# k of units 4 to 11 loaded in natural order and transposed by the DMA crossbar from SBUF to SBUF; the first unit's casts on VectorE; a new order by swaps

## The chip, the core and the metric

The kernel runs on one core of a Trainium2 chip. The metric is the device time of one execution in microseconds (us), as the median of several runs. Engines are named as in the profile: PE is TensorE's matmuls (PEld its weight loads), DVE is VectorE, ACT is ScalarE, POOL is GpSimd, and SP (SyncE) issues nearly all DMAs.

## The reference

Sliding-window attention with four sink positions, followed by a channel mix. The batch is 4, with 8 heads, 768 positions and a head size of 64; the mix works on 512 channels with 1024 hidden ones.

```python
scores = scale * np.matmul(q, k.transpose(0, 1, 3, 2))
keep = is_sink | in_window            # 4 sinks, window of 128
a = softmax(np.where(keep, scores, -1e9))
x = np.matmul(a, v)                   # heads side by side: [B, S, 512]
xk = mu_k * x + (1 - mu_k) * x_prev   # x_prev: one position earlier
xr = mu_r * x + (1 - mu_r) * x_prev
out = sigmoid(xr @ w_r) * (np.maximum(xk @ w_k, 0) ** 2 @ w_v)
```

## The kernel before

The work is cut into 12 units of 256 positions: unit u is batch u // 3, third T = u % 3. All matmuls are in bf16.

`load` brings k, q and v of a unit into SBUF in float32. k and q come as one DMA of 512 KB, with two neighbouring positions (j = 0, 1) side by side on a partition; unit 0's come as two DMAs of 256 KB. v comes as two DMAs of 256 KB in natural order, 128 positions on the 128 partitions.

`prepare` works on halves of four heads. k is cast to bf16 on ACT (`kb`), q on DVE (`qb`), by the table `CAST`. PE then makes four transposes of 128 x 128 into a PSUM bank (line 519), and ACT copies them from there into `kt` or `qt`, putting the positions back in order (line 527). v is cast on POOL (on DVE in unit 0) into `vb`. For the first unit of a batch, POOL copies the sink keys out of `kt`, and PE and DVE prepare the sink values.

`attend` makes two pairs of scores per unit (line 602), ACT takes the exponential (`e`, line 622), DVE applies the mask (line 636), PE multiplies by the values (lines 647 and 659), and DVE divides into `x`. A pair of scores reads the half of `kt` and `qt` with its heads, and that of the unit before. `mix` transposes x on PE (line 698), ACT copies it out (`xt`, line 704), and DVE makes `xk` and `xr`. `ffn` has, per unit, eight groups of key matmuls (line 740), ACT's relu (`rl`, line 749), the square on DVE (`kk`), two gates (line 763) with ACT's tanh (`th`), four groups of products (line 778), DVE's last step (`ob`, line 787) and two stores (line 794).

Each operation is recorded in a `Plan` with an engine, a planner's cost, what it reads and writes, and the buffers it takes and holds. The table `ORDER` lists, for each engine, the numbers of its operations in the order in which they are issued; numbers count the operations as they are recorded. `schedule` walks through those lists, hands out the buffers (three tiles of `kt`, two of `kb`, three of `ks`, four banks), and puts dummy matmuls (fills, line 798) into PE's queue up to a planned time of 45 us where it plans a gap. Every engine works through its list in order, so an instruction that waits holds up all behind it. SP's list holds the loads and the stores.

Of the kernel before, what the change touches and what calls it, by code (L numbers as in the profile page):

```python
# [18 lines left out]

TOGETHER = 2  # L20
# [34 lines left out]
    ),  # L55
    "DVE": (
# [23 lines left out]
    ),  # L80
    "ACT": (
# [14 lines left out]
    ),  # L96
    "POOL": (
        61, 60, 63, 64, 65, 62, 90, 127, 128, 179, 180, 261, 259, 340, 260, 341, 420, 421, 500,
        501, 581, 582, 661, 662, 502, 741, 743, 822, 742, 902, 823, 903,
# [10 lines left out]
class Plan:  # L110
# [23 lines left out]
    def schedule(self):  # L134
# [42 lines left out]
        while any(lines.values()):  # L177
# [35 lines left out]
            if o["service"]:  # L213
# [4 lines left out]
                k = 0  # L218
# [46 lines left out]
def kernel(  # L265
# [60 lines left out]
    def dve(n, rate=1.04):  # L326
        return 64.0 + rate * n

    def act(n):
        return 67.0 + 0.833 * n  # L330
# [240 lines left out]
    def attend(u, rank):  # L571
# [33 lines left out]
        def made(name, w, c):  # L605
            return [(name, w, c // 2)]
# [243 lines left out]
```

## Time and profile before

| | |
|---|---|
| median of 3 runs | 183.73 us (183.46 to 183.82) |
| profiled execution | 183.11 us |
| its span, first to last instruction | 181.3 us |
| granted PE clock, mean | 0.979 |
| HBM read, written | 24.12 MB, 6.29 MB |

In a row of the profile, the line of the kernel, the engine and the operation come first, then what is written and read, the number of instructions, and their busy time with the mean of one. The part after the bar is the time that the engine stood idle just before them, with what ended it. A timeline row has the start, the time taken, and the idle time before it in square brackets. PE's matmuls overlap in these rows: what one takes from PE is the step from start to start.

### The profile page before, as it was taken

To read this page: it belongs to the slowest core of one execution; us is meant where nothing else is said; L and a number is where in the kernel's file an instruction comes from. 1 tells how busy PE (TensorE), PEld (TensorE's weight loads), DVE (VectorE), ACT (ScalarE), POOL (GpSimd) and SP (SyncE) were. 2 spreads that over 40 slices of the span, in tenths; PEclk is the share of its full clock that TensorE was granted. 3 is DMA by queue.
4 is the path that set the end of the run, shared out by engine and by line. 5 is a ranking of instruction groups with operands and counts; after the bars stand their busy time and mean duration, and the time that the engine had idled before them with its cause. 6 is when DMAs were issued, how large, how long until landed. Compare 5 with 4: busy or idle time off the path is not lost.

```text
span 181.3 us, 4366 instructions
## 1 busy us (share of the span) xinstructions
PE 169.3 (93%) x1687; PEld 114.2 (63%) x1710; DVE 152.9 (84%) x389; ACT 139.0 (77%) x225; POOL 23.2 (13%) x47
## 2 busy tenths in 40 slices
PE   7997689889999999999999999999999999999991
PEld 2444358545857858677658668658568668756640
DVE  6127699999989999979988999989989999997531
ACT  3097589798899994999999989888899958723321
POOL 6200120012510001170023000003300100000000
PEclk9999759999999999999999999999999999999999
DMA  4999999999785999829997215058006004011032
GB/s 109 269 285 310 333 306 346 336 215 282 190 216 157 319 263 269 212 49 264 292 160 204 86 63 174 4 124 227 4 0 177 0 0 175 2 52 63 5 124 107
DMA packets 57124, 30.69 MB, mean 169 GB/s; under 512 B 26896, under 2 KB 51472, under 8 KB 57104
## 3 DMA queue, kind: packets, MB, share of 16 engines
q1 hardware_dynamic: 56048, 30.41, 62.0%
q8 instruction: 13, 0.21, 0.5%
q10 hardware_dynamic: 1056, 0.00, 0.3%
q14 instruction: 7, 0.06, 0.1%
HBM read 24.12 MB, written 6.29 MB: 168 GB/s over the span
## 4 chain that ended last, share of the span: by engine, by line
PE 73%; DVE 19%; ACT 4%; issue 2%; DVEq 0%
PE bank L778 20%; PE bank L740 18%; PE bank L763 10%; PE sc L602 6%; PE bank L798 5%; PE bank L659 5%; PE bank L519 5%; DVE xk L719 3%; PE bank L698 3%; DVE xr L719 3%; DVE e L636 2%; DVE x L675 2%; PE bank L647 2%; DVE kk L753 2%; ACT e L622 2%
## 5 line engine op out<-in xcount | busy, mean ns | idle before, releaser
L740 PE MATMUL bank<-xk,wk_sb 128*128 128x256 bf16 x384 | 51.9, 274 | 0.7 <-ACT th L769 0.4
L778 PE MATMUL bank<-wv_h,kk 128*128 128x512 bf16 x179 | 47.0, 379 | 0.7 <-issue 0.2
L622 ACT ACTIVATE e<-sc 128x1024 bf16<-128x1024 f32 (+1 forms) x48 | 44.8, 963 | 1.0 <-PE sc L602 0.9
L740 PEld LDWEIGHTS <-wk_sb 128*128 128x128 bf16 x384 | 35.5, 98 | 8.5 <-issue 1.0
L749 ACT ACTIVATE rl<-bank 128x512 bf16<-128x512 f32 x48 | 27.9, 608 | 13.5 <-PE bank L740 6.5
L636 DVE TENSOR_TENSOR e<-e,mask 128x1024 bf16<-128x1024 bf16 (+1 forms) x48 | 30.6, 645 | 3.8 <-ACT e L622 3.7
L542 POOL CAST vb<-vs 128x512 bf16<-128x512 f32 x22 | 17.0, 795 | 77.3 <-DMA vs<-in_v_dram 73.6
L778 PEld LDWEIGHTS <-kk 128*128 128x128 bf16 x192 | 17.4, 98 | 14.4 <-issue 0.3
L763 PE MATMUL bank<-wr_sb,xr 128*128 128x512 bf16 x87 | 23.7, 379 | 0.5
L787 DVE SCALAR_TENSOR_TENSOR ob<-th,bank 128x512 f32<-128x512 f32 x24 | 16.4, 682 | 9.0 <-PE bank L778 4.5
L719 DVE SCALAR_TENSOR_TENSOR xk<-td,mu,xt 128x256 bf16<-128x256 bf16 x48 | 23.3, 502 | 0.2
L719 DVE SCALAR_TENSOR_TENSOR xr<-td,mu,xt 128x256 bf16<-128x256 bf16 x48 | 23.3, 497 | 0.1
L527 ACT COPY qt<-bank 128x512 bf16<-128x512 bf16 x24 | 17.9, 744 | 7.0 <-PE bank L519 6.9
L659 PE MATMUL bank<-vb,e 128*128 128x65 bf16 x352 | 19.9, 193 | 1.5 <-DVE e L636 1.1
L753 DVE TENSOR_TENSOR kk<-rl 128x512 bf16<-128x512 bf16 x48 | 19.8, 425 | 1.5 <-ACT rl L749 1.5
L675 DVE TENSOR_TENSOR x<-bank,rec 128x256 bf16<-128x256 f32 x48 | 19.8, 418 | 0.7
L659 PEld LDWEIGHTS <-e 128*128 128x128 bf16 x352 | 17.1, 97 | 5.0 <-DVE e L636 1.4
L527 ACT COPY kt<-bank 128x512 bf16<-128x512 bf16 x24 | 17.8, 743 | 2.6 <-PE bank L519 2.6
L704 ACT COPY xt<-bank 128x512 bf16<-128x512 bf16 x24 | 14.1, 587 | 6.4 <-PE bank L698 6.2
L769 ACT ACTIVATE th<-bank 128x512 f32<-128x512 f32 x24 | 14.1, 606 | 4.0 <-PE bank L763 4.0
L507 ACT CAST kb<-ks 128x512 bf16<-128x512 f32 x24 | 14.7, 629 | 1.4 <-DMA ks<-in_k_dram 1.4
L602 PE MATMUL sc<-qt,kt 64*128 64x128 bf16 (+1 forms) x256 | 14.7, 248 | 0.9 <-ACT kt L527 0.8
(46 smaller groups left out, 165.9 us busy)
## 6 DMA issues: line engine op xcount, KB each, us to landing
vs<-in_v_dram SPq DMA_DIRECT2D x24, 256.0 KB, 5.8
out_dram<-ob SPq DMA_DIRECT2D x24, 256.0 KB, 2.9
qs<-in_q_dram SPq DMA_DIRECT2D x11, 512.0 KB, 6.1
ks<-in_k_dram SPq DMA_DIRECT2D x11, 512.0 KB, 5.7
wk<-in_moe_w_k_dram SPq DMA_DIRECT2D x2, 1024.0 KB, 9.1
wv<-in_moe_w_v_dram SPq DMA_DIRECT2D x2, 1024.0 KB, 11.3
wr<-in_moe_w_r_dram SPq DMA_DIRECT2D x1, 1024.0 KB, 8.5
ks<-in_k_dram SPq DMA_DIRECT2D x2, 256.0 KB, 4.0
```

The source lines that it names most:

```text
L527: nc.scalar.copy(out=buf[key][:, 2 * half:2 * half + 2, :, :].rearrange("p c g (t j) -> p c j (g t)", j=2), in_=buf[psk].bitcast(BF16)[:, ...
L602: nc.tensor.matmul(out=sc[:, a, o0:o1], lhsT=lhs[rows], rhs=rhs[rows], start=True, stop=True)
L622: nc.scalar.activation(out=buf[ek][:, :, lo:], in_=buf[sck][:, :, lo:], func=AF.Exp, scale=scale)
L636: nc.vector.tensor_tensor(out=at, in0=at, in1=m, op=ALU.mult)
L659: nc.tensor.matmul(out=o[:, g, a, :], lhsT=e[:, a, e0:e0 + 128], rhs=rhs, start=(T == 0 and i == 0), stop=(i == len(blocks) - 1), skip_gro ...
L675: P.op("DVE", dve(256), lambda ok=ok, rk=rk, c=c: nc.vector.tensor_tensor(out=buf["x", u][:, :, 128 * c:128 * c + 128].rearrange("p g (a d ...
L719: nc.vector.scalar_tensor_tensor(out=buf[key][:, c0 + i, :], in0=buf[tk][:, i, :], scalar=mu[w][:, c0 + i:c0 + i + 1], in1=xt[:, c0 + i, t ...
L740: nc.tensor.matmul(out=ps[:, i, :], lhsT=wk_sb[:, c, 128 * f:128 * f + 128], rhs=xk[:, c, :], start=(c == 0), stop=(c == NC - 1), skip_gro ...
L749: P.op("ACT", act(512), lambda psk=psk, rk=rk: nc.scalar.activation(out=buf[rk], in_=buf[psk].rearrange("p (i t) -> p i t", i=2), func=AF. ...
L753: P.op("DVE", dve(512, 0.52), lambda f2=f2, rk=rk: nc.vector.tensor_tensor(out=buf["kk", u][:, 2 * f2:2 * f2 + 2, :], in0=buf[rk], in1=buf ...
L763: nc.tensor.matmul(out=buf[psk], lhsT=buf["xr", u][:, c, 128 * g:128 * g + 128], rhs=wr_sb[:, c, :], start=(c == 0), stop=(c == NC - 1))
L778: nc.tensor.matmul(out=buf[psk], rhs=wv_h[:, f, :], lhsT=buf["kk", u][:, f, 128 * g:128 * g + 128], start=(f == 0), stop=(f == NF - 1))
```

## The change

- k of units 4 to 11 (`KD`) is loaded in natural order, like v, by two DMAs of 256 KB (the halves are now blocks of 128 positions, not groups of heads). ACT casts each half into `kb` without a reordering, and a transposing DMA, issued on SP, writes it into `kt` (128 x 512 bf16, four blocks of 128 x 128). PE's transposes and ACT's copies of these halves are gone: 16 groups of four transposes and 16 copies. The DMA's reads and writes are both in SBUF.
- All scores of a unit whose k comes that way read both halves of `kt` (`made`).
- In unit 0, k's casts and the copies of q's transposes are done on DVE, no longer on ACT (`CAST0`, `EVAC0`).
- `schedule` starts each engine's planned clock at a given time (`BEGIN`) and plans fills in the first 4 us at 430 ns each.
- `ORDER` is a new table for all engines.

```diff
+CAST0 = {"k": "DVE", "q": "DVE"}
+EVAC0 = {"k": "ACT", "q": "DVE", "x": "ACT"}
+KD = range(4, 12)
+QD = ()
+BEGIN = {"SP": 800.0, "PE": 1260.0, "ACT": 2600.0, "DVE": 930.0, "POOL": 930.0}
...
     "PE": (
-        77, 80, 93, 83, 86, 104, 96, 119, 101, 107, 125, 129, 122, 112, 116, 145, 136, 91, 171,
+        88, 85, 101, 91, 94, 112, 127, 124, 104, 109, 115, 137, 120, 153, 99, 130, 144, 185,
...
-                while t - now > 300.0 and now < self.fill_until:
+                while t - now > (300.0 if now > 4000.0 else 600.0) and now < self.fill_until:
...
-                    now += 225.0
+                    now += 225.0 if now > 4000.0 else 430.0
...
+    def by_dma(name, u):
+        return u in (KD if name == "k" else QD)
...
+            if by_dma(name, u):
+                for g in range(2):
+                    s0 = 256 * T + 128 * g
+                    P.op("SP", 980.0, lambda key=key, src=src, g=g, s0=s0: nc.sync.dma_start(
+                        out=buf[key][:, 4 * g:4 * g + 4, :, :].rearrange("p h j d -> p (h j) d"),
+                        in_=src[b, :, s0:s0 + 128, :].rearrange("h p d -> p h d")), rank,
...
-            by = CAST[name]
+            by = (CAST if u else CAST0)[name]
...
+                     out=buf[rk][:, half, :, :].rearrange("p h d -> p (h d)"),
+                     in_=buf[raw][:, hs, :, :].rearrange("p h j d -> p (h j d)"))
+                 if by_dma(name, u) else copy(
...
+            if by_dma(name, u):
+                P.op("SP", 1200.0, lambda key=key, rk=rk, half=half: nc.sync.dma_start_transpose(
+                    out=buf[key][:, :, half, :],
+                    in_=buf[rk][:, half, :, :].rearrange("p h d -> p (h d)")), rank + half,
...
+                continue
...
+            by = "ACT" if u else EVAC0[name]
...
+            if by_dma(name[0], w):
+                return [(name, w, 0), (name, w, 1)]
             return [(name, w, c // 2)]
```

How the new table moves instructions is shown at three places. The number after a name is that of its buffer: `ks1` is the second of three tiles for loaded k, `kt2` the third of three for transposed k.

The start, SP's queue: the first eight DMAs before.

```order
L358 DMA ks0_67<-in_k_dram 128x4x128
L358 DMA qs0_70<-in_q_dram 128x4x128
L358 DMA ks0_67<-in_k_dram 128x4x128
L350 DMA vs0_73<-in_v_dram 128x8x64
L358 DMA qs0_70<-in_q_dram 128x4x128
L358 DMA qs1_71<-in_q_dram 128x8x128
L350 DMA vs0_73<-in_v_dram 128x8x64
L358 DMA ks1_68<-in_k_dram 128x8x128
```

And the first eight now.

```order
L378 DMA ks0_67<-in_k_dram 128x4x128
L378 DMA qs0_70<-in_q_dram 128x4x128
L378 DMA ks1_68<-in_k_dram 128x8x128
L378 DMA ks0_67<-in_k_dram 128x4x128
L378 DMA qs0_70<-in_q_dram 128x4x128
L361 DMA vs0_73<-in_v_dram 128x8x64
L378 DMA qs1_71<-in_q_dram 128x8x128
L361 DMA vs0_73<-in_v_dram 128x8x64
```

Unit 1's k (`ks1`) has moved from the eighth place to the third, ahead of the second half of unit 0's k and q. The first half of `w_k`, ninth before, is now twelfth.

The start, DVE's queue after its memsets: before.

```order
L507 CAST qb0_78<-qs0_70 128x4x2x64
L542 CAST vb0_115<-vs0_73 128x8x64
L507 CAST qb0_78<-qs0_70 128x4x2x64
L636 TENSOR_TENSOR e1_86<-e1_86,mask0_125 128x2x384
L507 CAST qb1_79<-qs1_71 128x4x2x64 x2
L636 TENSOR_TENSOR e0_85<-e0_85,mask0_125 128x2x384
```

Now.

```order
L530 CAST qb0_78<-qs0_70 128x4x2x64
L561 COPY qt0_83<-bank0_63 128x2x2x128
L530 CAST kb0_76<-ks0_67 128x4x2x64
L530 CAST qb0_78<-qs0_70 128x4x2x64
L672 TENSOR_TENSOR e0_85<-e0_85,mask0_125 128x2x384
L530 CAST kb0_76<-ks0_67 128x4x2x64
L576 CAST vb0_115<-vs0_73 128x8x64
L561 COPY qt0_83<-bank2_65 128x2x2x128
```

DVE now casts k and copies q's transposes of unit 0 out of the bank, one half ahead of its first mask (the `TENSOR_TENSOR` on `e`) and one behind it. On PE, in the same place, 13 fills instead of 19 stand ahead of the first transposes; q's come first now, then five fills, then k's, then four fills, then unit 0's first scores.

The middle, ACT's queue around the preparation of unit 5 (whose k is in `kb1` and `kt2`, whose q goes to `qt1`): before, around the two copies into `kt2`.

```order
L527 COPY kt2_82<-bank2_65 128x2x2x128
L704 COPY xt1_134<-bank0_63 128x2x256
L527 COPY qt1_84<-bank0_63 128x2x2x128
L749 ACTIVATE rl2_107<-bank0_63 128x512
L704 COPY xt1_134<-bank1_64 128x2x256
L749 ACTIVATE rl0_105<-bank2_65 128x512
L749 ACTIVATE rl1_106<-bank3_66 128x512
L527 COPY qt1_84<-bank1_64 128x2x2x128
L527 COPY kt2_82<-bank2_65 128x2x2x128
L622 ACTIVATE e1_86<-sc1_62 128x1024
```

Now, from unit 4's first exponential to the second cast of unit 5's k.

```order
L658 ACTIVATE e1_86<-sc0_61 128x1024
L787 ACTIVATE rl0_105<-bank3_66 128x512
L527 CAST kb1_77<-ks2_69 128x512
L658 ACTIVATE e0_85<-sc1_62 128x1024
L620 ACTIVATE es0_89<-bank1_64 128x256
L742 COPY xt1_134<-bank3_66 128x2x256
L787 ACTIVATE rl1_106<-bank0_63 128x512
L658 ACTIVATE e2_87<-sc1_62 128x1024
L807 ACTIVATE th0_108<-bank1_64 128x512
L807 ACTIVATE th1_109<-bank3_66 128x512
L527 CAST kb1_77<-ks2_69 128x512
```

No copy into `kt2` is left on ACT; the casts of unit 5's k stand among unit 4's exponentials. On PE there stand, between the end of unit 4's first pair of scores and unit 5's: nine groups of keys, one sink group, four products, two gates, one pair of scores, three groups of transposes and three of values (one of them of a first unit of a batch, half as long).

The middle, SP's queue around unit 5's two transposing DMAs, now.

```order
L371 DMA ks2_69<-in_k_dram 128x8x64
L378 DMA qs2_72<-in_q_dram 128x8x128
L361 DMA vs2_75<-in_v_dram 128x8x64
L378 DMA qs0_70<-in_q_dram 128x8x128
L538 DMA_TRANSPOSE kt2_82<-kb1_77 128x4x128
L371 DMA ks0_67<-in_k_dram 128x8x64
L538 DMA_TRANSPOSE kt2_82<-kb1_77 128x4x128
L371 DMA ks0_67<-in_k_dram 128x8x64
L378 DMA qs1_71<-in_q_dram 128x8x128
L361 DMA vs2_75<-in_v_dram 128x8x64
```

Before, SP's queue held only loads and stores. The second transposing DMA of unit 5 now stands ahead of loads for the units 6 and 7 and of the second half of unit 5's v.

More of the change, by code (lines that the diff above doesn't have):

```diff
@@ L34 @@
     "PE": (
[20 rows of a table removed]
[19 rows of a table added]
     ),
     "DVE": (
[23 rows of a table removed]
[23 rows of a table added]
     ),
     "ACT": (
[14 rows of a table removed]
[13 rows of a table added]
     ),
     "POOL": (
-        61, 60, 63, 64, 65, 62, 90, 127, 128, 179, 180, 261, 259, 340, 260, 341, 420, 421, 500,
-        501, 581, 582, 661, 662, 502, 741, 743, 822, 742, 902, 823, 903,
+        69, 71, 68, 72, 135, 73, 98, 70, 136, 187, 188, 267, 268, 346, 269, 347, 424, 425, 502,
+        503, 504, 581, 582, 659, 660, 737, 816, 739, 738, 894, 895, 817,
     ),
     "SP": (
[4 rows of a table removed]
[6 rows of a table added]
     ),
@@ L171, in schedule @@
             at[i] = 0.0
-        clock, port, dma, flying, mode = {}, {}, 0.0, [], 0
+        clock, port, dma, flying, mode = dict(BEGIN), {}, 0.0, [], 0
         released = {key: 0.0 for key in owner}
@@ L356, in load @@
             src = {"k": k, "q": q}[name]
+            if by_dma(name, u):
[4 more added lines that the diff above has]
+                        in_=src[b, :, s0:s0 + 128, :].rearrange("h p d -> p h d")), rank,
+                        service=1320.0, descs=1024, take=[] if g else [(name + "s", key)],
+                        hold=[key] if g else [], writes=[(name, u, g)])
+                continue
             P.op("SP", 128 * (h1 - h0) * 0.9 + 60.0, lambda key=key, src=src: nc.sync.dma_start(
@@ L503, in prepare @@
             hs = slice(4 * half, 4 * half + 4)
-            by = CAST[name]
+            by = (CAST if u else CAST0)[name]
             copy = nc.scalar.copy if by == "ACT" else nc.vector.tensor_copy
             P.op(by, act(512) if by == "ACT" else dve(512, 0.52),
-                 lambda copy=copy, raw=raw, rk=rk, hs=hs: copy(
+                 lambda copy=copy, raw=raw, rk=rk, hs=hs, half=half, name=name: copy(
+                     out=buf[rk][:, half, :, :].rearrange("p h d -> p (h d)"),
+                     in_=buf[raw][:, hs, :, :].rearrange("p h j d -> p (h j d)"))
+                 if by_dma(name, u) else copy(
                      out=buf[rk][:, :, hs, :].rearrange("p j h d -> p h j d"),
@@ L512, in prepare @@
                  writes=[rk + (half,)])
+            if by_dma(name, u):
+                P.op("SP", 1200.0, lambda key=key, rk=rk, half=half: nc.sync.dma_start_transpose(
+                    out=buf[key][:, :, half, :],
+                    in_=buf[rk][:, half, :, :].rearrange("p h d -> p (h d)")), rank + half,
+                    service=1030.0, descs=512, reads=[rk + (half,)],
+                    take=[] if half else [(name + "t", key)],
+                    hold=[rk] + ([key] if half else []), writes=[key + (half,)])
+                continue
             def transpose(half=half, psk=psk, rk=rk):
@@ L524, in prepare, with evacuate @@
                  reads=["ident", rk + (half,)], writes=[psk], hold=[rk])
-            def evacuate(half=half, psk=psk, key=key):
-                nc.scalar.copy(
+            by = "ACT" if u else EVAC0[name]
+            def evacuate(half=half, psk=psk, key=key, by=by):
+                (nc.scalar.copy if by == "ACT" else nc.vector.tensor_copy)(
                     out=buf[key][:, 2 * half:2 * half + 2, :, :].rearrange(
@@ L531, in evacuate @@
                         "p (c j t) -> p c j t", c=2, j=2))
-            P.op("ACT", act(512) + 160.0, evacuate, rank + half,
+            P.op(by, act(512) + 160.0 if by == "ACT" else dve(512), evacuate, rank + half,
                  hold=[psk] + ([key] if half else []),
@@ L703, in mix @@
                  reads=["ident", ("x", u, c0), ("x", u, c0 + 1)], writes=[psk])
-            P.op("ACT", act(512), lambda c0=c0, psk=psk: nc.scalar.copy(
+            by = "ACT" if u else EVAC0["x"]
+            copy = nc.scalar.copy if by == "ACT" else nc.vector.tensor_copy
+            P.op(by, act(512) if by == "ACT" else dve(512), lambda c0=c0, psk=psk, copy=copy: copy(
                 out=xt[:, c0:c0 + 2, t0:t0 + 256],
```

120 rows, old and new, of the table ORDER are left out of this document.

## The prediction

> **What bounds the kernel now.** I read the page's busy shares first, then the chain that ended last, then the busy time by stretch.
>
> ```profile
> span 181.3 us, 4366 instructions
> PE 169.3 (93%) x1687; PEld 114.2 (63%) x1710; DVE 152.9 (84%) x389; ACT 139.0 (77%) x225; POOL 23.2 (13%) x47
> PE 73%; DVE 19%; ACT 4%; issue 2%; DVEq 0%
> ```
>
> TensorE (PE) carries 73% of the chain, VectorE (DVE) 19%. These are averages over two stages, which the view by stretch parts (columns: stretch, its length, then busy us of PE, PEld, DVE, ACT, POOL, the granted clock, DMA share, GB/s):
>
> ```profile
> 0.00:12.70 12.70, 11.39 (x58) 5.08 (x60) 4.08 (x16) 5.29 (x8) 4.10 (x17) 1.00 0.95 212
> 12.70:20.00 7.30, 5.01 (x61) 2.96 (x58) 5.17 (x15) 5.78 (x10) 1.26 (x3) 1.00 1.10 327
> 20.00:30.00 10.00, 8.38 (x83) 6.03 (x84) 9.12 (x21) 7.49 (x12) 1.19 (x1) 0.66 1.04 320
> 30.00:46.00 16.00, 14.19 (x135) 9.25 (x135) 15.94 (x37) 13.50 (x24) 1.97 (x2) 1.00 1.09 283
> 46.00:90.00 44.00, 43.52 (x496) 31.20 (x502) 41.92 (x112) 39.86 (x67) 8.12 (x11) 1.00 0.85 222
> 90.00:150.00 60.00, 59.44 (x648) 42.06 (x656) 56.33 (x143) 53.76 (x89) 6.55 (x13) 1.00 0.37 95
> ```
>
> From 30 to 46 us DVE is idle for 0.06 us and PE for 1.8: DVE sets the pace. From 46 to 150 PE is idle for 1.0 of 104 us, DVE for 2.1 + 3.7 = 5.8, ScalarE (ACT) for 10.4: PE sets it. So PE work taken out after 46 us is worth its full length until DVE's 5.8 us are used up.
>
> **Transposes and evacuations of k, units 4 to 11.** The groups of instructions (busy us, mean ns | idle before) and three consecutive PE rows of the timeline (start, us):
>
> ```profile
> L519 PE MATMUL bank<-ident,kb 128*128 128x128 bf16 x96 | 9.3, 219 | 0.3 <-ACT qt L527 0.3
> L527 ACT COPY kt<-bank 128x512 bf16<-128x512 bf16 x24 | 17.8, 743 | 2.6 <-PE bank L519 2.6
> L507 ACT CAST kb<-ks 128x512 bf16<-128x512 f32 x24 | 14.7, 629 | 1.4 <-DMA ks<-in_k_dram 1.4
> 105.42 0.39 PE L519 MATMUL bank<-ident,kb 128*128 128x128 bf16 x4
> 105.64 0.39 PE L519 MATMUL bank<-ident,qb 128*128 128x128 bf16 x4
> 105.86 0.81 PE L778 MATMUL bank<-wv_h,kk 128*128 128x512 bf16 x3
> ```
>
> The mean of 219 ns overlaps with its neighbours; what a group of four takes from PE is the step to the next start, 0.22 us. Sixteen of the 24 groups go, all in the PE-bound stage: 16 x 0.22 = **-3.5 us**. ACT loses 16 x 0.743 = 11.9 us there, worth nothing by itself, because ACT was idle for 10.4 us already, but it gives the casts room. The k casts stay at 0.63 us each: the natural order changes their addresses, not their 512 elements, and ACT's freed time covers a slower one.
>
> **The crossbar transfers that replace them.** No row shows one. The nearest are these (KB each, median us from issue to landing; then the queue's own longest wait):
>
> ```profile
> vs<-in_v_dram SPq DMA_DIRECT2D x24, 256.0 KB, 5.8
> out_dram<-ob SPq DMA_DIRECT2D x24, 256.0 KB, 2.9
> ks<-in_k_dram SPq DMA_DIRECT2D x11, 512.0 KB, 5.7
> SPq L794 <- DVE ob L787: 63.3, 11, 12.0
> ```
>
> A half of k is 128 KB. It could land sooner than a store's 2.9 us, or as late as a load's 5.8, or later, since a crossbar may be slower than a copy. What matters is the **lead**: from the end of ACT's cast of a unit's second half to the start of that unit's first scores, which now need both halves. Unit 5, from the orders shown above and these lengths:
>
> ```profile
> 46.42 0.44 PE bank L740 x4
> 52.02 0.86 PE bank L778 x4
> 58.44 0.44 PE bank L578 x4
> 58.88 0.55 PE sc L602 x12
> 64.00 0.86 PE bank L763 x4
> 131.70 0.37 PE bank L659 x12
> L622 ACT ACTIVATE e<-sc 128x1024 bf16<-128x1024 f32 x32 | 32.4, 1034 | 0.3 <-PE sc L602 0.2
> L749 ACT ACTIVATE rl<-bank 128x512 bf16<-128x512 f32 x48 | 27.9, 608 | 13.5 <-PE bank L740 6.5 <-issue 4.1 <-DVE xk L719 1.6
> L704 ACT COPY xt<-bank 128x512 bf16<-128x512 bf16 x24 | 14.1, 587 | 6.4 <-PE bank L698 6.2
> L586 ACT ACTIVATE es<-bank 128x256 bf16<-128x256 f32 x8 | 3.1, 388 | 1.1 <-PE bank L578 1.1
> ```
>
> Between unit 4's first scores and unit 5's, PE has 9 key groups (4.0 us), 4 products (3.4), 2 gates (1.7), one sink group (0.44), one pair of scores (0.55), three transposes (0.66) and three groups of values (I put each at 0.37 or less; about 0.9): 11.7 us. In the same time ACT has three exponentials (3.1), two relus, two tanhs (like the relus, 0.61) and one xt copy (3.0), one es (0.39) and two k casts (1.26): 7.8 us to the end of unit 5's second cast. Lead 3.9 us. The same count for the other seven units gives 3.8 to 5.4.
>
> A landing like the store's (2.9) fits every lead; one like a load's (5.8) fits none. I take a landing near the store's, 3 to 3.5 us: half the store's bytes, and no trip to HBM. For collisions with loads, most likely in units 4 to 7 where the DMA share is 0.85, I add **+0.6 us**, between nothing and the 5.8 - 3.9 = 1.9 us of one late landing. On SP's queue the 16 transfers and 8 extra k loads are 24 more issues, each waiting for its cast, and behind unit 5's second one stand the loads of q of unit 7 and the second v of unit 5; that queue waited 63.3 us for results to store, so issue time itself is hidden. The smaller k loads (256 KB, like those of v) are issued units ahead; ACT waited only 1.4 us for all k loads (the row of kb above). The copies of the sink keys of units 6 and 9 on POOL now wait for a DMA instead of ACT; POOL is 13% busy and their reader, the sink group of the next unit, comes a whole unit later.
>
> Two pages of the Trainium skill differ on this. "VectorE: DVE Perf Modes", § The three transpose paths, gives 390 ns to a 128 x 128 bf16 transpose on TensorE and 1309 ns through the crossbar, and its rules advise TensorE where PSUM will do; this trace has TensorE at 0.22 us for four, and by the page's figure a half of four blocks would take 5.2 us (estimate), beyond nearly every lead. "Advanced Engine Details and Errata", § X-Bar Transpose (TRN2), calls these transfers as fast as regular ones; by that they land like the store. No row of this trace decides.
>
> **The first stage.** Timeline rows of the start, and two DVE groups:
>
> ```profile
> 1.26 6.76 PE L798 MATMUL bank<-warm 128*128 128x512 bf16 x19 [1.26 <-DVE warm L813]
> 5.82 0.43 DVE L507 CAST qb<-qs 128x512 bf16<-128x512 f32 x1 [1.91 <-DMA qs<-in_q_dram]
> 10.56 0.50 PE L602 MATMUL sc<-qt,kt 64*128 64x256 bf16 x8
> 20.48 1.04 PE L602 MATMUL sc<-qt,kt 64*128 64x256 bf16 x12 [0.82 <-ACT kt L527]
> L507 DVE CAST qb<-qs 128x512 bf16<-128x512 f32 x24 | 9.8, 415 | 2.5 <-DMA qs<-in_q_dram 2.5
> L565 DVE TENSOR_TENSOR vsink<-bank,hmask 32x512 bf16<-32x512 f32 x4 | 2.7, 675 | 0.5 <-PE bank L561 0.5
> ```
>
> Before, 19 fills hold PE until 8.0 us although q is cast at 6.25. With 13 fills (6.76 / 19 = 0.36 us each in the mean, 0.43 at the slow start) PE is free between 5.9 and 6.8. Then four q transposes, q's copy on DVE (0.42 to 0.68; a PSUM read stands nearest to the 0.675 row), k's cast (0.42), four k transposes, k's copy on ACT (0.74), with about 0.1 us from engine to engine: first scores near 9.7 instead of 10.56, **-0.8**. DVE gains 2 casts and 2 copies, 2 x 0.42 + 2 x 0.65 = 2.1 us; the first pair lies in its idle time before 12.7 us (busy 4.08), the second, 1.1 us, in the DVE-paced stage. Against that, DVE was idle for 2.1 us from 12.7 to 20 and 0.9 from 20 to 30, while unit 1's scores waited for kt until 20.48; its k is now the third load, not the eighth. Between none and all of these 3.0 us, the stage ends between 0.3 us later (+1.1 - 0.8) and 2.7 earlier. I take **-1.0 us** in all: the added DVE work is paid for and 1.3 of the 3.0 idle us are found (-0.8 + 1.1 - 1.3). The weights land later, but their first use stands later in PE's order too.
>
> **Sum**, against the profiled execution, 183.11 us (span 181.3 and 1.8 around it): -3.5 - 1.0 + 0.6 = -3.9, so 179.2. The median of the three runs, 183.73, stands 0.6 above that execution; I forecast **179.7 us** as the median after.
>
> **Rivals.**
> - *DVE takes the bound.* DVE's work after 46 us stays while the stage gets shorter by 3.5, so its idle time would fall from 5.8 to 2.3 of about 100 us. For: it was 84% busy in all and paced 30 to 46. Against: there it ran with 0.06 us idle in 16. If half the PE gain is lost: 183.11 - 1.8 - 0.5 + 0.6 = 181.4, about 182.0 as a median (181 to 183.6).
> - *The transfers land late: slower.* PE then waits at the first scores of each of eight units for landing minus lead. With leads of about 4.6, 3.9, 4.7, 5.1, 5.4, 5.2, 3.8, 3.8 the waits add up to 4.5 us, the whole gain, at a landing of about 5 us: that is the point from which it decides. At 5.8 they are 9.9: 183.7 - 4.5 + 9.9 = 189.1. For: all loads take 5.7 or more, and the crossbar is unseen (the 5.2 us of the page above falls here). Against: 2.9 for the store, and a share of 0.37 after 90 us.
> - *The first stage gives more.* All 3.0 us of early DVE idle time found: 2.7 instead of 1.0, 178.0 as a median (177 to 178.5). For: unit 1's wait at 20.48 and the clock of 0.66 from 20 to 30, which PE's idle time there may cause. Against: the loads before 30 us run at a share above 1.0, so what comes sooner pushes something else back.
>
> **Chances.** Forecast 0.51 (178.5 to 181), DVE 0.18, late transfers 0.22, first stage 0.09. The range 177 to 187 leaves out a little below and the worse half of the late transfers. A measurement here can tell about 0.2% (0.37 us) from no change. Faster takes the forecast, the first stage and most of the DVE case (0.14): 0.74. Slower takes 0.20 of the late transfers; the rest, 0.06, is within.
>
> **What would show it.** Right: no PE row waits for a DMA that writes kt; transfers land within 3.8 us of issue; ACT's busy time falls by some 14.6 us (11.9, and unit 0's two casts and two copies); the kb group of PE has 32 matmuls where it had 96; first scores before 10 us. Wrong: idle PE ahead of scores with the releaser kt's DMA (late transfers), DVE idle below 1 us from 46 us on with PE waiting for it (DVE), first scores of unit 2 no earlier than before. What would upset the forecast most is a landing above 5 us.

## The result, and the profile after

| | before | after |
|---|---|---|
| median, run side by side, first comparison | 183.77 us (183.46 to 184.40, 4 runs) | 177.85 us (176.89 to 178.66, 4 runs) |
| median, run side by side, second comparison | 183.66 us (183.02 to 184.57, 23 runs) | 177.24 us (176.47 to 179.66, 6 runs) |
| profiled execution | 183.11 us | 178.66 us |

The ratio is 0.9671 (95% interval 0.9616 to 0.9727) in the first comparison and 0.9637 (0.9602 to 0.9672) in the second: 6 us, where 4.0 were forecast. Medians and ranges hold all runs of a kernel; ratios leave out those over 1.5% above its fastest. The profiled execution of after is the slowest of its four; it is 4.45 us below that of before.

The page of after, its span, busy shares and chain:

```profile
span 177.0 us, 4245 instructions
PE 164.5 (93%) x1619; PEld 109.8 (62%) x1640; DVE 154.3 (87%) x393; ACT 127.4 (72%) x205; POOL 25.1 (14%) x47
...
PE 71%; DVE 17%; DMA 3%; SPq 3%; issue 2%; ACT 1%; ACTq 0%; DVEq 0%
```

The same engines with the same shares: PE is at 93% still, of a span 4.3 us shorter, and DVE has come up from 84 to 87%. By stretch (length, busy us of PE, PEld, DVE, ACT, POOL, granted clock, DMA share, GB/s):

```profile
0.00:12.70 12.70, 11.26 (x63) 4.85 (x66) 6.84 (x23) 4.25 (x5) 3.42 (x14) 1.00 0.82 209
12.70:20.00 7.30, 4.40 (x67) 2.79 (x62) 6.09 (x19) 6.54 (x10) 2.91 (x7) 1.00 1.12 286
20.00:30.00 10.00, 8.25 (x97) 6.51 (x98) 8.87 (x23) 7.19 (x12) 0.00 (x0) 0.66 1.06 373
30.00:46.00 16.00, 14.96 (x127) 10.31 (x128) 15.60 (x35) 14.34 (x25) 4.74 (x3) 1.00 1.00 261
46.00:90.00 44.00, 43.13 (x484) 29.77 (x488) 43.00 (x112) 37.39 (x63) 7.21 (x12) 1.00 0.92 204
90.00:150.00 60.00, 59.47 (x634) 41.34 (x641) 58.14 (x151) 46.80 (x76) 6.87 (x11) 1.00 0.71 150
```

From 46 to 150 us PE is idle for 0.87 + 0.53 = 1.4 us (before 1.0) and DVE for 1.0 + 1.9 = 2.9 (before 5.8): PE still sets the pace, DVE is close behind. The groups that answer to those shown of before, and the transfers (KB, median us to landing):

```profile
L551 PE MATMUL bank<-ident,kb 128*128 128x128 bf16 x32 | 3.4, 232 | 0.5 <-DVE ob L825 0.2
L561 ACT COPY kt<-bank 128x512 bf16<-128x512 bf16 x8 | 5.9, 735 | 8.6 <-PE bank L551 8.6
L527 ACT CAST kb<-ks 128x512 bf16<-128x512 f32 x16 | 10.1, 632 | 0.0
L561 DVE COPY qt<-bank 128x512 bf16<-128x512 bf16 x2 | 1.5, 730 | 1.6 <-PE bank L551 1.6
kt<-kb SPq DMA_TRANSPOSE x16, 3.1
out_dram<-ob SPq DMA_DIRECT2D x24, 256.0 KB, 2.5
```

The kb group of PE has 32 matmuls, the casts in natural order take 0.63 us as before, and a crossbar transfer of 128 KB lands 3.1 us after its issue in the median, where the store of 256 KB takes 2.5. The sixteen are spread widely (shortest, median and longest):

```profile
DMA to landing us min/median/max: 2.4/3.1/5.6
```

The start, on DVE, PE and the small DMAs that ACT issues:

```profile
4.69 0.43 DVE L530 CAST qb<-qs 128x512 bf16<-128x512 f32 x1 [0.79 <-DMA qs<-in_q_dram]
8.63 0.50 PE L636 MATMUL sc<-qt,kt 64*128 64x256 bf16 x8
9.74 0.42 ACTq L412 DMA_DIRECT2D mu<-in_moe_mu_r_dram  x1
12.35 0.40 ACTq L412 DMA_DIRECT2D mu<-in_moe_mu_k_dram  x1
17.14 0.61 PE L636 MATMUL sc<-qt,kt 64*128 64x256 bf16 x12
```

q is cast at 4.69 us (before 5.82), the first scores stand at 8.63 (10.56), unit 1's at 17.14 (20.48). How far PE has come at 46 us is read from its weight loads (PEld) up to there, since the matmul rows of products and gates miss a few records (181 of 192 for the products of after). Of before and then of after, for keys, products and gates:

```profile
L740 PEld LDWEIGHTS <-wk_sb 128*128 128x128 bf16 x60 | 5.6, 101 | 2.0 <-issue 0.7 <-DVE wk_sb L484 0.2
L778 PEld LDWEIGHTS <-kk 128*128 128x128 bf16 x16 | 1.5, 97 | 1.4 <-issue 0.2
L763 PEld LDWEIGHTS <-xr 128*128 128x128 bf16 x8 | 0.8, 98 | 0.9
```

```profile
L778 PEld LDWEIGHTS <-wk_sb 128*128 128x128 bf16 x64 | 6.5, 103 | 3.2 <-DVE wk_sb L504 1.4
L816 PEld LDWEIGHTS <-kk 128*128 128x128 bf16 x16 | 1.5, 98 | 1.0
L801 PEld LDWEIGHTS <-xr 128*128 128x128 bf16 x12 | 1.2, 97 | 1.5 <-DVE xr L757 0.6
```

After has done four more key matmuls by then (0.44 us, as the prediction's row of four) and four more gates (0.86): 1.3 us, and with a few values, sink matmuls and transposes an estimated 1.8. The two terms, 3.5 and 1.8, would make 5.3 us; the spans differ by 4.3. Of the 1.0 between them, 0.4 is PE's added idle time from 46 to 150 us, and the rest isn't accounted for.

### The profile page after: what moved, and what is told of

Same layout as the page of the kernel before. It is cut to its first block, busy times and chain, and to the rows that moved or that the text cites. A ratio compares the mean times of both kernels' runs of the same rounds, so it can differ in the third digit from the quotient of the medians.

```text
span 177.0 us, 4245 instructions
## 1 busy us (share of the span) xinstructions
PE 164.5 (93%) x1619; PEld 109.8 (62%) x1640; DVE 154.3 (87%) x393; ACT 127.4 (72%) x205; POOL 25.1 (14%) x47
## 3 DMA queue, kind: packets, MB, share of 16 engines
q10 hardware_dynamic: 1056, 0.00, 0.3%
## 4 chain that ended last, share of the span: by engine, by line
PE 71%; DVE 17%; DMA 3%; SPq 3%; issue 2%; ACT 1%; ACTq 0%; DVEq 0%
PE bank L778 21%; PE bank L816 21%; PE bank L801 10%; PE bank L695 6%; PE sc L636 5%; DMA qs<-in_q_dram 3%; DVE xk L757 3%; DVE e L672 3%; PE bank L551 3%; PE bank L734 2%; DVE xr L757 2%; PE bank L683 2%; SPq L378 2%; DVE kk L791 2%; PE bank L612 2%
## 5 line engine op out<-in xcount | busy, mean ns | idle before, releaser
L658 ACT ACTIVATE e<-sc 128x1024 bf16<-128x1024 f32 (+1 forms) x48 | 45.4, 966 | 3.8 <-PE sc L636 3.7
L576 POOL CAST vb<-vs 128x512 bf16<-128x512 f32 x22 | 17.9, 822 | 103.5 <-DMA vs<-in_v_dram 90.2
L672 DVE TENSOR_TENSOR e<-e,mask 128x1024 bf16<-128x1024 bf16 (+1 forms) x48 | 31.1, 652 | 0.5 <-ACT e L658 0.5
L791 DVE TENSOR_TENSOR kk<-rl 128x512 bf16<-128x512 bf16 x48 | 20.8, 448 | 3.5 <-ACT rl L787 3.0
L757 DVE SCALAR_TENSOR_TENSOR xk<-td,mu,xt 128x256 bf16<-128x256 bf16 x48 | 22.4, 486 | 0.1
L695 PEld LDWEIGHTS <-e 128*128 128x128 bf16 x352 | 17.6, 100 | 3.3 <-DVE e L672 1.1
L561 ACT COPY qt<-bank 128x512 bf16<-128x512 bf16 x22 | 16.4, 748 | 1.6 <-PE bank L551 1.3
L801 PEld LDWEIGHTS <-xr 128*128 128x128 bf16 x96 | 9.0, 98 | 8.7 <-DVE xr L757 0.6
L683 PE MATMUL bank<-vsink,es 128*128 128x130 bf16 x64 | 13.3, 229 | 0.0
```

Of the source, the lines that this page charges most:

```text
L576: lambda g=g, copy=copy: copy(out=buf["vb", u][:, g, :, 0:D], in_=buf["v", u][:, g, :, :]), rank,
L658: nc.scalar.activation(out=buf[ek][:, :, lo:], in_=buf[sck][:, :, lo:], func=AF.Exp, scale=scale)
L672: nc.vector.tensor_tensor(out=at, in0=at, in1=m, op=ALU.mult)
L695: nc.tensor.matmul(out=o[:, g, a, :], lhsT=e[:, a, e0:e0 + 128], rhs=rhs, start=(T == 0 and i == 0), stop=(i == len(blocks) - 1), skip_gro ...
L757: nc.vector.scalar_tensor_tensor(out=buf[key][:, c0 + i, :], in0=buf[tk][:, i, :], scalar=mu[w][:, c0 + i:c0 + i + 1], in1=xt[:, c0 + i, t ...
L791: P.op("DVE", dve(512, 0.52), lambda f2=f2, rk=rk: nc.vector.tensor_tensor(out=buf["kk", u][:, 2 * f2:2 * f2 + 2, :], in0=buf[rk], in1=buf ...
```

## The experiments

Three questions: is PE's saved time the gain, what would late transfers have cost, and what did the start give? Times are medians; after stands for 177.24 us (ratio 0.9637) or 177.85 (0.9671), as above.

### The changed kernel again

> The changed kernel once more, beside the next three, so that they have their like on the same chip. Expected 177.9 us (176.9 to 178.7), 5.9 us below the kernel before.

177.24 us (176.47 to 179.66), as expected; this is the second comparison of the table.

### PE's transposes put back, with a bank of their own

```diff
                     hold=[rk] + ([key] if half else []), writes=[key + (half,)])
+                def dead(half=half, psk=psk, rk=rk):
+                    ps = buf[psk].bitcast(BF16)[:, 0:512].rearrange("p (c t) -> p c t", c=4)
+                    for c in range(4):
+                        nc.tensor.transpose(out=ps[:, c, :], identity=ident, in_=...)
+                P.op("PE", 225.0, dead, rank + half, lag=PE_LAG, take=[("bank", psk)],
+                     reads=["ident", rk + (half,)], writes=[psk], hold=[rk])
                 continue
```

> The changed kernel, with the 16 groups of four transposes of k put back on PE as dead work (no reader, no copy on ACT); the crossbar still writes kt. Theory (from 46 to 150 us PE sets the pace, so each 0.22 us taken from it counts whole): 3.5 us slower than the changed kernel, about 181.4. Rival (DVE has taken the bound there, and PE would have room): 0 to 1.5 us slower, 177.9 to 179.4.

Measured: 183.28 us (182.10 to 184.19), ratio 0.9969 (0.9949 to 0.9990): 6.0 us above after, more than either theory gave. DVE had no room to hide it, so the rival falls, but 6.0 is not 3.5. PE's waits from 46 us on (us in total, times, longest):

```profile
PE bank L549 <- DVE x L722: 1.3, 1, 1.3
PE bank L562 <- DVE ob L836: 0.2, 1, 0.2
PE bank L789 <- DVE x L722: 0.2, 1, 0.2
```

And in after:

```profile
PE bank L778 <- DVE ob L825: 0.4, 1, 0.4
```

With the dead groups PE waits 1.7 us, where after has 0.4, for DVE to be done with a bank: each dead group takes one of the four banks. The next run leaves the bank out.

### PE's transposes put back, without a bank

Four dead transposes go into the unused half of the bank that x's transposes of units 4 to 11 take anyway.

```diff
-                for i in range(2):
-                    for g in range(2):
-                        nc.tensor.transpose(out=ps[:, i, 128 * g:128 * g + 128], ...)
+                for n in range(2 if u in KD else 1):
+                    at = buf[psk].bitcast(BF16)[:, 512 - 512 * n:1024 - 512 * n]
+                    ps = at.rearrange("p (c t) -> p c t", c=2) if u in KD else ps
+                    for i in range(2):
+                        for g in range(2):
+                            nc.tensor.transpose(out=ps[:, i, 128 * g:128 * g + 128], ...)
```

> The changed kernel with 16 groups of four dead transposes on PE again, but these take no bank of their own: after the transposes of x of units 4 to 11, four more go into the unused half of the same bank. Theory (PE's time is what the groups cost; the further 2.5 us that the earlier version with them lost are waits for banks): 3.5 us slower than the changed kernel, about 180.8 (180.2 to 181.4). Rival (DVE bounds the stage, and that version lost its 6 us to banks alone): under 1.5 us slower, below 178.8.

Measured: 181.08 us (179.79 to 181.30), ratio 0.9831 (0.9798 to 0.9865). Against after's two ratios that is 0.0160 to 0.0194 of 183.8, or 2.9 to 3.6 us (1.7 to 4.5 with the intervals of both). The theory holds, and the rival's 1.5 us are too few: sixteen groups at 0.22 us are the price. The 2.2 us between this run and the one before are put down to the banks and the places that the dead groups took there; the trace showed 1.3 of them as added waits, the rest isn't shown. The stage looks like after's, with the added work in it:

```profile
46.00:90.00 44.00, 43.39 (x487) 30.23 (x491) 42.98 (x112) 37.22 (x61) 7.54 (x12) 1.00 0.96 204
90.00:150.00 60.00, 59.56 (x652) 42.30 (x657) 57.51 (x147) 46.11 (x75) 6.94 (x11) 1.00 0.63 149
```

PE is idle for 0.61 + 0.44 us in 104. The same run says what is left without PE's saving: 1 - 0.9831 of 183.8 is 3.1 us (2.5 to 3.7) below before, from the start, the new order, and the banks and copies that stay free.

### The crossbar alone, in the old order

The lines as they differ from the changed kernel:

```diff
-CAST0 = {"k": "DVE", "q": "DVE"}
-EVAC0 = {"k": "ACT", "q": "DVE", "x": "ACT"}
+CAST0 = {"k": "ACT", "q": "DVE"}
+EVAC0 = {"k": "ACT", "q": "ACT", "x": "ACT"}
-BEGIN = {"SP": 800.0, "PE": 1260.0, "ACT": 2600.0, "DVE": 930.0, "POOL": 930.0}
+BEGIN = {}
 (ORDER: the table of before, k's loads, casts and transfers of units 4 to 11 placed anew)
```

> The kernel before with nothing but the crossbar for k of units 4 to 11: its start, its fills, its casts and its order of all other work stay; the second casts of units 9 and 11, which stood behind those units' first scores, come earlier, and the new loads and transfers are put where they fit. Theory (PE's 16 groups are worth 3.5 us wherever the order comes from, the rest of the gain is the start's): 180.2 us, 179.8 to 181.2. Rival (without the new order the transfers and SP's queue hold PE up): 183 us or more.

Measured: 182.85 us (181.69 to 185.66), ratio 0.9936 (0.9903 to 0.9969), between the two theories. One place held it down. Three rows of its timeline, on SP, ACT and PE:

```profile
92.45 2.83 SPq L371 DMA_DIRECT2D ks<-in_k_dram  x2
99.35 0.62 ACT L527 CAST kb<-ks 128x512 bf16<-128x512 f32 x1 [2.50 <-DMA ks<-in_k_dram]
100.52 0.60 PE L778 MATMUL bank<-xk,wk_sb 128*128 128x256 bf16 x4 [2.23 <-ACT rl L787]
```

ACT's cast of unit 9's k waits 2.5 us for loads that SP issued from 92.45 us on, behind others; the relu behind that cast is late, and PE stands still for 2.23 us. So the load was moved:

```diff
 (SP's list)
-q of unit 10, v of unit 8, v of unit 7, k of unit 9, k of unit 9
+v of unit 7, k of unit 9, v of unit 8, k of unit 9, q of unit 10
```

(The load of v of unit 7 still stands ahead of both loads of k.)

> The kernel before with the crossbar alone, once more, but unit 9's two loads of k stand ahead of three loads on SP (those of v of units 7 and 8 and q of unit 10). Theory (the 2.2 us that PE waited behind ACT's cast for that load are what held the gain down): 2.2 us faster than the first such version, 180.6. Rival (the old order loses it somewhere else): 182 or more.

Measured: 181.30 us (180.78 to 181.50), ratio 0.9856 (0.9827 to 0.9885): 2.6 us (2.1 to 3.2) below before. The wait has gone; from 90 to 150 us PE is idle for 1.1 us:

```profile
90.00:150.00 60.00, 58.91 (x639) 41.11 (x647) 57.57 (x147) 47.89 (x77) 7.20 (x13) 1.00 0.65 141
```

So the crossbar alone brings most of PE's 3.5 us even in the old order, once its loads stand early enough, and late loads at one place cost 1.5 us by the two medians (182.85 and 181.30), 2.2 as the wait in the trace. From here to after there are 0.9856 - 0.9671 and 0.9856 - 0.9637 of 183.8, or 3.4 to 4.0 us: the start and the new order, this time from the other side.

### Late transfers: the transfer doubled

```diff
-                P.op("SP", 1200.0, lambda ...: nc.sync.dma_start_transpose(
+                P.op("SP", 1200.0, lambda ...: [nc.sync.dma_start_transpose(
                     out=buf[key][:, :, half, :],
-                    in_=buf[rk][:, half, :, :].rearrange("p h d -> p (h d)")), rank + half,
+                    in_=buf[rk][:, half, :, :].rearrange("p h d -> p (h d)"))
+                    for _ in range(1 + half)], rank + half,
```

> The changed kernel, with the transposing DMA of each unit's second half issued twice, the second after the first, so that the half is complete only about 6.2 us (two landings of 3.1) after the first issue. Theory (the landings fit by about 2 us, and this is all that keeps the change on the good side): with the distances from issue to first scores of the trace (6.2, 5.1, 5.4, 7.8, 5.65, 6.1, 5.0, 5.5 us) PE waits 1.1 + 0.8 + 0.55 + 0.1 + 1.2 + 0.7 = 4.5 us in all, about 182.4. Rival (waits at scores are taken back by the slack around them): under 1 us slower, at most 178.9.

Measured: 192.29 us (191.27 to 193.26), ratio 1.0458 (1.0414 to 1.0503): 15 us above after, three times the theory. PE's, SP's and ACT's waits:

```profile
PE sc L637 <- DMA kt<-kb: 2.6, 2, 1.6
```

```profile
SPq L538 <- DMA kt<-kb: 13.5, 8, 2.7
```

```profile
ACT kb L527 <- DMA ks<-in_k_dram: 10.0, 4, 4.3
```

The scores themselves wait for kt for 2.6 us in all. But the second transfer stands in SP's queue until the first has landed, 13.5 us in eight places, loads behind it are late, and ACT waits 10.0 us for k to cast, where after shows no such wait. The run tests a held queue more than a late landing.

### Late transfers: POOL delays the readers

```diff
+                if half:
+                    def later(key=key):
+                        for _ in range(4):
+                            nc.gpsimd.tensor_copy(out=buf[key][:, :, 1, :],
+                                                  in_=buf[key][:, :, 1, :])
+                    P.op("POOL", 3000.0, later, rank + 1, hold=[key], writes=[key + (1,)],
+                         port=False)
                 continue
```

> The changed kernel with each unit's last half of kt copied onto itself four times by POOL after it has landed, so that scores may read it some 3 us later, while SP's queue is left as it is (the doubled transfer held that queue too). Theory (late landings cost landing minus lead, unit by unit): with 3 us the shortages are 4.5 us, about 181.8 in all; were it 2 us, 1 us or less. Rival (one late landing also makes all that stands behind it on PE and ACT late, as in the run with the doubled transfer): 185 or more.

Measured: 187.41 us (186.61 to 187.88), ratio 1.0188 (1.0151 to 1.0225): about 10 us above after. It isn't a clean test either. The stretch from 90 us on, POOL's copies, DVE's mask (0.652 us in after) and two waits of PE:

```profile
90.00:150.00 60.00, 56.65 (x587) 37.43 (x591) 59.56 (x140) 46.50 (x74) 22.53 (x32) 1.00 0.72 158
```

```profile
L548 POOL COPY kt<-kt 128x512 bf16<-128x512 bf16 x32 | 24.6, 770 | 41.6 <-DMA kt<-kb 36.2 <-PE bank L787 3.9
```

```profile
L681 DVE TENSOR_TENSOR e<-e,mask 128x1024 bf16<-128x1024 bf16 (+1 forms) x48 | 33.3, 698 | 1.0 <-ACT e L667 1.0
```

```profile
PE bank L704 <- POOL vb L585: 3.1, 1, 3.1
PE sc L645 <- POOL kt L548: 0.4, 2, 0.2
```

The scores wait for POOL's copies for 0.4 us only. But DVE's mask takes 7% longer in this run, DVE is idle for 0.44 us from 90 to 150 (after: 1.9), and PE for 3.35: this is what the stage looks like when DVE takes the bound, and in after it doesn't look so. A late cast of v on POOL adds 3.1 us, ahead of that stretch. What a late landing by itself costs, with every queue left alone, was not measured.

### More of the same: q by the crossbar too

```diff
-QD = ()
+QD = range(8, 12)
-            by = (CAST if u else CAST0)[name]
+            by = "ACT" if name == "q" and by_dma(name, u) else (CAST if u else CAST0)[name]
 (ORDER: found anew after 36 us)
```

> The changed kernel with q of units 8 to 11 by the crossbar as well (its casts on ACT, in natural order, 8 more transposing groups and copies gone from PE and ACT), where the DMA share is lower; the order after 36 us is found anew. Theory (PE still sets the pace after 46 us, each group taken out is worth its 0.22 us, and DVE gives 8 x 0.42 us of casts away): 8 x 0.22 = 1.8 us faster than the changed kernel, 175.7 (175.0 to 176.4). Rival (16 more transfers and loads make SP's queue late and scores wait, or ACT with its casts does): 177.3 or more.

Measured: 180.88 us (178.97 to 181.49), ratio 0.9820 (0.9780 to 0.9861): better than before, but 3 us worse than after. PE's waits in the profiled execution, its fastest:

```profile
PE sc L635 <- DMA kt<-kb: 1.8, 1, 1.8
PE sc L635 <- DMA qt<-qb: 0.4, 1, 0.4
90.00:150.00 60.00, 57.33 (x587) 39.12 (x594) 55.79 (x140) 45.30 (x76) 8.71 (x11) 1.00 0.81 174
```

Here the transfers do come late: scores wait 2.2 us for them, and PE is idle for 2.67 us from 90 to 150, at a DMA share of 0.81 where after has 0.71. The rival's sign is right. The trace accounts for what the eight groups would have brought (1.8 us), not for all of the 3 us: its other runs were up to 2.5 us slower than this one, and have no trace. The order after 36 us is another one too, and what that costs or brings wasn't taken apart.

### The start: mu's small DMAs, unit 1's k, the granted clock

```diff
 (ACT's list: mu's two DMAs first)
-86, 107, 102, 64, 92, 63, ...
+64, 63, 86, 107, 102, 92, ...
```

> The changed kernel with the two tiny DMAs of mu (2 KB each, 1056 packets) first in ACT's queue again, as in the kernel before, where they were issued at 0.81 us; in the changed kernel they come after 9 us. Theory (they crowd the first loads, and their move is what let q land 1.1 us earlier): q's first cast starts near 5.8 instead of 4.7, first scores 9.7 instead of 8.6, the end 0 to 1.1 us later. Rival (the order of SP's first loads did it): no change, 177.2.

Measured: 178.09 us (176.94 to 178.90), ratio 0.9674 (0.9636 to 0.9712). Its start:

```profile
0.81 0.48 ACTq L412 DMA_DIRECT2D mu<-in_moe_mu_r_dram  x1
1.31 0.60 ACTq L412 DMA_DIRECT2D mu<-in_moe_mu_k_dram  x1
5.94 0.43 DVE L530 CAST qb<-qs 128x512 bf16<-128x512 f32 x1 [2.03 <-DMA qs<-in_q_dram]
9.16 0.50 PE L636 MATMUL sc<-qt,kt 64*128 64x256 bf16 x8
```

SP's list is that of after, and yet q is cast at 5.94 instead of 4.69 (4.64 in the second profile of after). So two DMAs of 2 KB, issued beside the first loads, make q land 1.25 us later: the theory holds for the landing. Of that, 0.53 us reach the first scores (9.16 for 8.63), and the end can't be told from after's. The kernel before isn't quite the same case: only the first of the two went out that early there (0.81 us), the other at 4.02.

```diff
 (SP's list)
-k 0, q 0, k 1, k 0, q 0, v 0, q 1, v 0
+k 0, q 0, k 0, q 0, v 0, q 1, v 0, k 1
```

> The changed kernel with unit 1's load of k put back from the third place on SP to the eighth, as in the kernel before. Theory (its early load is what brings unit 1's first scores from 20.5 to 17.1 us and with them most of the 1.75 us that the start gained): first scores of unit 1 after 19.5, the end 1 to 2 us later, 178.5 to 179.5. Rival (the start gained by DVE's order and the earlier first scores): under 0.5 us later, 177.7 or less.

Measured: 178.72 us (177.98 to 178.73), ratio 0.9718 (0.9686 to 0.9750), 0.9 to 1.5 us above after by the ratios; its interval overlaps one of after's two and not the other, and its profiled execution, 177.98 us, is below after's 178.66. So the size is unclear; that the median lies in the expected 178.5 to 179.5 is luck, for the mechanism isn't the expected one:

```profile
17.52 0.67 PE L636 MATMUL sc<-qt,kt 64*128 64x256 bf16 x12
```

Unit 1's scores come 0.4 us later than in after, not 2.4. The early load isn't what brings them forward from 20.48.

```diff
+    def keep_warm(emit, key, n):
+        def both():
+            emit()
+            for _ in range(n):
+                nc.tensor.matmul(out=buf[key][:, 272:512], lhsT=warm[:, 0:128],
+                                 rhs=warm[:, 0:240], start=True, stop=True,
+                                 skip_group_check=True)
+        return both
 (after: 10 behind the second xt group of unit 0, 10 behind the second values of unit 1;
  before: 33 behind five groups of units 0 and 1)
```

> The changed kernel with ten short dummy matmuls behind PE's last work before each of its two long idle stretches of the start (18.5 to 20.0 us and 24.2 to 25.8 us), written into unused halves of banks that are held anyway. Theory (the spread of the changed kernel, 176.5 to 179.7 us, is PE's granted clock, which drops to 0.5 for some microseconds after 17 to 27 us in some runs and not in others; its fastest runs have a mean clock of 0.998): with PE kept busy the clock stays, all runs near 176.7 (176.3 to 177.0). Rival (the spread comes from the loads, and dummy work only delays PE): 177.2 or more, as wide as before.

> The kernel before with the same kind of dummy matmuls in its idle stretches between 15.8 and 23.5 us (33 in five places). Theory (its runs all have a mean clock of 0.971 to 0.981, so each of them has the drop, at the price of some 2 us that the changed kernel pays in some runs only; that is part of the 6 us between the medians): about 181.7, with a clock near 0.998. Rival (DVE and the loads pace its start, so the clock costs it nothing): 183.7.

Measured: after with the dummy work 177.65 us (177.32 to 179.65), ratio 0.9693 (0.9648 to 0.9737); before with it 184.71 us (183.67 to 185.28), ratio 1.0052 (1.0024 to 1.0079). The stretch from 20 to 30 us of the two:

```profile
20.00:30.00 10.00, 8.09 (x113) 6.08 (x114) 9.96 (x26) 8.55 (x14) 0.00 (x0) 1.00 1.06 374
```

```profile
20.00:30.00 10.00, 6.94 (x90) 5.43 (x91) 8.20 (x19) 7.73 (x12) 1.25 (x1) 1.00 1.02 308
```

The granted clock is 1.00 where it was 0.66 in both kernels, and neither ratio is lower for it; before is 0.4 to 1.4 us slower. So the clock as a cause of the 6 us between the kernels falls. As a cause of the spread it is open. In the ten runs of after, the mean clock and the time go together (0.999 and 0.998 in runs of 176.47 and 176.79 us, 0.977 and 0.981 in those of 178.66 and 179.66). With the dummy work all six had 0.995 to 1.00; five took 177.3 to 177.8 and one 179.65, none the expected 176.3 to 177.0. In the runs with the late k, 178.72 us came at a clock of 1.00 and 177.98 at 0.978. Whether a low clock makes a run late, or late work lowers the clock, isn't shown. What paces that stretch instead is suggested by the rows, not tested: DVE is busy for 9.96 of 10 us in the one, and the DMA share is 1.02 in the other.

## Why the prediction was right, and where it was off

The sign and the range of 177 to 187 held. The forecast of 179.7 was some 2 us too high: the medians, 177.2 and 177.9, lie outside its own band of 178.5 to 181, in the band of the rival that was given a chance of 0.09 (*the first stage gives more*, 177 to 178.5). The mechanism of the largest term was right; the first stage was mis-sized. For the profiled execution the sum gave 179.2, and 178.66 came; that this is so near is in part luck, since a larger first stage and 1.0 us lost later cancel there.

- **PE's 16 groups, -3.5.** Right, and shown from two sides: 2.9 to 3.6 us when the work is put back without a bank, 2.6 (2.1 to 3.2) when the crossbar comes alone. Put back with a bank it cost 6.0, which neither theory nor rival of that run foresaw. PE sets the pace before and after, as the stretches say.
- **The landing, 3 to 3.5 us.** Right in the median: 3.1. But six of the sixteen missed the sign of 3.8 us, with 3.9 to 5.6. Each of the six was issued over 7 us ahead of its unit's first scores, and no row of PE waits for a DMA that writes kt. The reading that all loads take 5.7 us or more was wrong: the first two loads of k, 256 KB each, landed after 4.0. Of the two pages of the Trainium skill, "Advanced Engine Details and Errata", § X-Bar Transpose (TRN2), is the nearer: the transfer of 128 KB lands close to a store of 256 KB (2.5). The estimate of 5.2 us from "VectorE: DVE Perf Modes", § The three transpose paths, isn't borne out for a whole transfer of four blocks, in the median; two of the sixteen took longer than that (5.4 and 5.6).
- **The leads, 3.8 to 5.4.** All eight were longer, 5.0 to 7.8 us. Unit 5's was put at 3.9; it is 5.0, from the issue at 65.25 us, right behind the cast, to the scores at 70.27. PE's work between came out as counted (11.8 us from the end of unit 4's first scores), ACT's took 6.8 instead of 7.8:

```profile
65.25 1.20 SPq L538 DMA_TRANSPOSE kt<-kb  x1
70.27 0.62 PE L636 MATMUL sc<-qt,kt 64*128 64x256 bf16 x12
```

- **Late landings, +0.6.** Nothing of it is to be seen: no wait of PE on kt. PE's idle time from 46 to 150 grew by 0.4 us, put down to DVE's last step, not to transfers.
- **The first stage, -1.0.** This is the term that was mis-sized. PE's progress at 46 us is worth some 1.8 us in the profiled executions, and the medians give 3.1 (2.5 to 3.7, with the free banks and copies) from one side and 3.4 to 4.0 from the other for start and order together; what lies between 1.8 and these is in no trace. First scores were put at 9.7 and came at 8.63. The prediction took q's landing as given (cast at 5.82); it moved to 4.69, since mu's DMAs had left the start, a step of the new order that the prediction didn't count. That explains 0.5 us of the first scores; nothing of it can be told at the end. The prediction also let DVE find 1.3 of its 3.0 idle us between 12.7 and 30; by the rows it is idle for 1.2 + 1.1 there now, so only 0.7 were found, but before 12.7 us it did 2.76 us more (6.84 instead of 4.08), where the prediction had counted only the first added cast and copy, 1.1. By 46 us DVE has done 37.4 us of work (the sum of four stretches) where it had done 34.3, and only 2 x 0.41 + 2 x 0.73 = 2.3 of the 3.1 more were added.
- **ACT's busy time, -14.6.** The copies of kt give 11.9, as foreseen, but the page's total, in which overlapping instructions count once, fell by 11.6 only (139.0 to 127.4). The prediction took no account of overlap. Worth nothing by itself, as said; that wasn't tested.
- **Rivals.** DVE doesn't take the bound (2.9 us idle in 104, where 2.3 were foreseen). *The first stage gives more* has the time, but not by its mechanism: of DVE's 3.0 idle us from 12.7 to 30 only 0.7 were found, and raising the clock of 0.66 brought nothing. Late transfers were priced as landing minus lead. Neither run tested that price alone: what came with the lateness (a held queue with late loads in one, a slower DVE and a late cast on POOL in the other) cost 15 and 10 us where 4.5 were expected. That scores can wait for transfers is shown in the run with q by the crossbar too: 2.2 us, more than its eight groups would bring.

**What stays open.** The profiled executions show 4.45 us, the medians 5.9 to 6.4. The profiled executions of after are the slowest of their comparisons (178.66 and 179.66), and what makes the others 1 to 3 us faster is in no trace; PE's clock goes with it, but is not shown to be the cause. Nor were start and order taken apart: the old order with the new start was not run. What a late landing costs by itself is open too.

## What to carry to other kernels

Where one engine sets the pace of a stage, work taken off it is worth the step from start to start, not the busy time of its group; count banks and queue places that go with it, too. A transfer that takes over such work must be issued ahead of its reader by more than its median landing: here the landings went from 2.4 to 5.6 us, and 5.0 to 7.8 us of lead were enough. The loads and casts ahead of it must stand early in their queues: late loads at one place gave back 1.5 of 2.6 us. An edit that comes with a new order should have the first few microseconds priced anew, down to the smallest DMAs, even if here that moved the first scores and not measurably the end.

## What the runs showed of the hardware

- Two DMAs of 2 KB with 1056 packets between them, issued on another queue at 0.81 and 1.31 us, beside the first loads, made the first load of q land 1.25 us later (cast at 5.94 instead of 4.69 us).
- PE's granted clock of 0.66 from 20 to 30 us, raised to 1.00 by dummy matmuls, made neither kernel's ratio better (0.9693 beside 0.9671 and 0.9637 for after, 1.0052 for before).
- Sixteen transposing DMAs of 128 KB landed 2.4 to 5.6 us after their issue, 3.1 in the median, and kept the issuing queue for 1.2 us each in the median.
- In the run in which POOL copied 128 x 512 bf16 in SBUF 32 times (0.77 us each), DVE's mask took 0.698 us in the mean instead of 0.652.
